# Stores of finished rows: moved from SyncE's queue to ScalarE's, with a longer pause before them

## The chip, the core and the metric

The kernel runs on one core of a Trainium2 chip. The metric is the device time of one execution in microseconds (us), the median of several runs. The engines are named as in the profile: PE is TensorE, DVE is VectorE, ACT is ScalarE, POOL is GpSimd, and SP is SyncE, which computes nothing and here only issues DMAs.

## What is computed

The input `x` holds 4 sequences of 3584 rows with 192 channels. Three layers follow each other:

```python
out = einsum('hk,bskhg->bshg', softmax(weight), x_windows)   # causal filter, 7 taps, 8 heads of 24 channels
skip = x @ w_skip > 0                                        # only these rows pass the first expert layer
e = argmax(x @ w_gate); y = gate * (relu(x @ w1[e]) @ w2[e]) # 8 experts, 192 -> 1024 -> 192
x[skip] = x[skip] + y[skip]
e2 = argmax(x @ w_gate2 + modality_bias[modality_id])        # second expert layer, every row
out = gate2 * (relu(x @ w1b[e2]) @ w2b[e2])
```

## The kernel before

The 14336 rows are cut into 128 tiles of 112 rows, and 16 tiles make a group, so there are eight groups (`NG`). **Phase 1** works on the groups one after the other. For each group and each of the 8 heads TensorE multiplies the input with a band matrix (`filt`); ScalarE scales the result into the tile `hl` as f16 (`conv`, line 711), and VectorE adds the low part that the f16 lost (`lows`, line 724). TensorE transposes pairs of tiles (`tr`), ScalarE copies them to SBUF as `xtb`, and a second matmul (`gm`) gives the gate logits. When all logits of a group are there, `fin` (line 767) computes the expert codes and the gate factors on GpSimd and VectorE, with one exponential on ScalarE, and writes factors and row numbers into spare columns of `hl`. Then `store` (line 794) sends `hl` to the DRAM tensor `rows`, 112 partitions with 16 rows of 792 bytes each, 1386 KB a group.

`hl` is allocated in `conv` with `bufs=4`: the first conv of group g+4 writes into the buffer of group g and must wait until that group's store has read it.

**After and beside phase 1**, `route_a` turns the codes into lists of rows per expert, on VectorE, GpSimd and TensorE. `prep` splits the expert weights into f16 high and low parts on ScalarE and VectorE and writes them to DRAM; its lane 1 takes its SBUF from the memory that phase 1 gave back. `Ffn.run` then works through blocks of 128 rows of one expert: an indirect gather from `rows` (GpSimd), a DMA transpose (`xpose`, SP), two matmul stages, with `hh` (ScalarE) and `hlo` (VectorE) between them. Blocks of the first layer that need only groups 0 to 3 start while groups 5 to 7 still pass `fin` and `route_a`.

**The order of the work** is written out by hand. Every side job is a Python generator; `Tasks.tick` (line 98) advances each of them by one schedule step, and `yield n` means that the generator goes on n steps later. Phase 1 counts v from 0 to 75; in each v it makes a transpose, a `lows`, one step of all side jobs, a conv and a `gm`, and then a second step of the side jobs. `fin(g)` is added at v = 8g+19. During the blocks, `bg` (line 1292) gives the steps, two per call and four calls per block at first. For ScalarE, VectorE, TensorE and GpSimd the wrapper `InOrder` fixes the instructions in the order in which the program issues them. SP has no such wrapper: the scheduler may place its DMAs in another order.

```python
class Core:
    def __init__(self, tc):
        self.raw = tc.nc
        self.vector, self.scalar = InOrder(tc, tc.nc.vector), InOrder(tc, tc.nc.scalar)
        self.tensor, self.gpsimd = InOrder(tc, tc.nc.tensor), InOrder(tc, tc.nc.gpsimd)
```

Line 70 of the profile is the call inside `InOrder`, so nearly all instructions of the four engines carry it. Numbers such as conv(g,h) mean group and head.

Of the kernel before, what the change touches and what calls it, by code (L numbers as in the profile page):

```python
# [10 lines left out]
I32 = mybir.dt.int32  # L11
# [12 lines left out]
TP = 112  # L24
# [3 lines left out]
GT = 16  # L28
# [29 lines left out]
def f32v(t):  # L58
    return t.rearrange("p t c -> p (t c)").bitcast(F32).rearrange("p (t c) -> p t c", c=RW // 2)
# [600 lines left out]
class Phase1:  # L660
# [106 lines left out]
    def fin(self, g):  # L767
        nc, m, p = self.nc, self.m, self.p2
        t0 = g * GT
        L, hl, (s, inv) = self.L.pop(g), self.hl.pop(g), self.sc.pop(g)  # L770
        meta = f32v(hl)
        nc.gpsimd.tensor_copy(meta[:, :, MB + 2], inv[:TP, 0:1].to_broadcast([TP, GT]))
        nc.gpsimd.tensor_copy(meta[:, :, MB + 3], m.modf[:, t0:t0 + GT])
        nc.gpsimd.tensor_copy(meta[:, :, MB + 4], m.ids[:, t0:t0 + GT])
        nc.gpsimd.memset(meta[:, :, MB + 5], 0.0)
        sc17 = p.tile([TP, 17], F32, name="sc17")
        nc.gpsimd.tensor_tensor(sc17, m.gsi[:TP], inv[:TP, 0:1].to_broadcast([TP, 17]), ALU.mult)
        nc.gpsimd.tensor_tensor(L, L, sc17.unsqueeze(1).to_broadcast([TP, GT, 17]), ALU.mult)
        nc.gpsimd.tensor_tensor(L[:, :, 9:17], L[:, :, 9:17], m.bias[:, t0:t0 + GT, :], ALU.add)
        yield 4  # L780
        cd = p.tile([TP, GT, 2], F32, name="cd")
        gt = p.tile([TP, GT, 2], F32, name="gt")
        for w in m.gate(nc.gpsimd, L[:, :, 1:17].rearrange("p t (m e) -> p t m e", m=2), GT, 2, p, cd, gt, 2, 3, 1):
            yield w
        yield 1
        nc.vector.scalar_tensor_tensor(m.code[:TP, 0, t0:t0 + GT], L[:, :, 0], 0.0, cd[:, :, 0], ALU.is_gt, ALU.mult)
        nc.vector.scalar_tensor_tensor(m.code[:TP, 1, t0:t0 + GT], L[:, :, 0], 0.0, cd[:, :, 1], ALU.is_le, ALU.mult)
        nc.gpsimd.tensor_copy(meta[:, :, MB], gt[:, :, 0])
        nc.gpsimd.tensor_tensor(meta[:, :, MB + 1], gt[:, :, 1], inv[:TP, 0:1].to_broadcast([TP, GT]), ALU.mult)
        self.codes = g + 1  # L790
        yield 2
        self.store(g, meta)

    def store(self, g, meta):
        t0 = g * GT
        self.nc.sync.dma_start(self.rows[t0 * 128 + 128:(t0 + GT) * 128 + 128, :].rearrange("(p t) c -> p t c", p=128)[:TP], meta.bitcast(I32))

    def run(self, tk, tkw, tables):
        for g in range(2):
# [601 lines left out]
```

## Time and profile before

| what | value |
|---|---|
| median of 3 runs | 1024.06 us (1023.78 to 1024.61) |
| the profiled execution | 1022.52 us |
| its span in the trace | 1020.7 us |
| PE busy | 947.0 us (93%) |
| DVE busy | 640.6 us (63%) |
| ACT busy | 455.4 us (45%) |
| POOL busy | 523.9 us (51%) |
| mean granted TensorE clock | 0.969 |

The span runs from the first to the last recorded instruction; the execution's own time has 1.8 us more around it. Shares over the whole span mix phase 1 with the long stretch of blocks behind it, so stretches are read one by one. A granted clock of 1.00 is 2.4 GHz, 0.50 is 1.2 GHz.

### The profile page before, as it was taken

What the parts mean: (1) busy time and instruction counts of PE and PEld (TensorE: products, weight loads), DVE (VectorE), ACT (ScalarE), POOL (GpSimd) and SP (SyncE); (2) the same over time, 40 slices, a digit from 0 to 9 for tenths busy, and PEclk for the clock granted to TensorE, in tenths of its full rate; (3) what the DMA queues carried; (4) which work ended last, traced back from release to release, by engine and by line L of the source; (5) the groups of instructions that cost most, each with busy time, mean ns of one, the idle gap of its engine ahead of it and who ended that gap; (6) DMA issues with size and microseconds to landing.
All of it is one profiled execution on the core that took longest, in us unless ns stands there. A gap on an engine that the chain in (4) does not pass through costs nothing. (4 is left out here: it accounts for less than half of the span.)

```text
span 1020.7 us, 30001 instructions
## 1 busy us (share of the span) xinstructions
PE 947.0 (93%) x11512; PEld 881.3 (86%) x11512; DVE 640.6 (63%) x1742; ACT 455.4 (45%) x833; POOL 523.9 (51%) x1027
## 2 busy tenths in 40 slices
PE   5998968999999799998999999999999999999994
PEld 3666757989999789998889999998898999999994
DVE  6699975989989998875445555558633333333331
ACT  2786641525555334433355555543233333333331
POOL 4055788444443233344277877854354555555532
PEclk9999869999999999999899999999999999999997
DMA  8394768667888596669933434342276322223231
GB/s 290 146 336 184 236 218 229 194 199 206 238 253 231 154 316 192 187 187 283 304 77 105 107 88 120 97 112 68 55 245 174 72 71 75 73 76 75 75 96 45
DMA packets 109145, 165.53 MB, mean 162 GB/s; under 512 B 80975, under 2 KB 86073, under 8 KB 103232
## 3 DMA queue, kind: packets, MB, share of 16 engines
q1 hardware_dynamic: 94368, 134.02, 42.6%
q0 software_dynamic: 13920, 28.87, 11.7%
q8 instruction: 92, 1.51, 0.6%
q10 hardware_dynamic: 704, 0.63, 0.2%
q14 instruction: 61, 0.50, 0.2%
HBM read 181.56 MB, written 58.42 MB: 235 GB/s over the span
## 5 line engine op out<-in xcount | busy, mean ns | idle before, releaser
L70 PEld LDWEIGHTS <-w1b 128*128 128x128 f16 x4840 | 370.7, 99 | 35.4 <-issue 9.0
L70 DVE SCALAR_TENSOR_TENSOR ws<-bank,ws 128x512 f16<-128x512 f32 x220 | 151.9, 691 | 252.7 <-ACT ws L70 250.0
L70 PE MATMUL bank<-xp,w1b 128*128 128x256 f16 x2200 | 262.5, 273 | 3.1 <-DMA xp<-gt 2.0
L70 PEld LDWEIGHTS <-ws 128*128 128x128 f16 (+2 forms) x3088 | 248.1, 98 | 8.7 <-issue 2.2
L70 PE MATMUL bank<-w2b,ws 128*128 128x192 f16 x2640 | 239.2, 246 | 0.0
L70 POOL DMA_INDIRECT out_dram<-u,si x114 | 115.2, 1010 | 168.9 <-ACT u L70 109.2
L70 ACT ACTIVATE ws<-bank 128x512 f16<-128x512 f32 x220 | 130.6, 597 | 118.7 <-PE bank L70 117.9
L70 PE MATMUL bank<-xt,w1b 128*128 128x128 f16 x2640 | 167.7, 224 | 7.6 <-DVE hlo L70 4.4
L70 ACT ACTIVATE hh<-bank 128x512 f16<-128x512 f32 x132 | 78.2, 593 | 154.8 <-PE bank L70 148.3
L70 PE MATMUL bank<-w2b,hh 128*128 128x192 f16 x1056 | 140.7, 249 | 3.4 <-DMA w2b<-s2a 3.4
L70 PE MATMUL bank<-w2b,hlo 128*128 128x192 f16 x528 | 131.4, 249 | 0.0
L70 DVE SCALAR_TENSOR_TENSOR hlo<-bank,hh 128x512 f16<-128x512 f32 x132 | 90.0, 685 | 49.0 <-ACT hh L70 48.6
L70 POOL DMA_INDIRECT gt<-rows,idxs x44 | 48.2, 1096 | 137.0 <-issue 116.0
L70 ACT ACTIVATE u<-bank,c 128x192 f32<-128x192 f32 x114 | 47.9, 420 | 145.9 <-PE bank L70 121.3
L70 PEld LDWEIGHTS <-hh 128*128 128x128 f16 x1056 | 96.0, 101 | 4.1 <-issue 3.7
L70 POOL DMA_INDIRECT gt<-rows,idx x64 | 63.8, 997 | 28.2 <-issue 15.5
L70 POOL DMA_INDIRECT gt<-rows,idxB x56 | 55.9, 998 | 26.9 <-issue 12.5
L70 PE MATMUL bank<-xg,band 128*112 128x384 f32 x128 | 60.0, 559 | 4.2 <-DVE hl L70 4.2
L70 POOL TENSOR_TENSOR xs<-gt 128x128 f32<-128x128 f16 x124 | 53.6, 457 | 6.7 <-DVE x2s L70 4.8
L70 PE MATMUL bank<-ob,oa 128*128 128x56 f16 (+2 forms) x446 | 49.8, 263 | 5.1 <-DVE ob L70 3.9
L70 ACT COPY xtb<-bank 128x672 f16<-128x672 f16 x64 | 45.9, 720 | 16.7 <-PE bank L70 16.4
L70 PEld LDWEIGHTS <-hlo 128*128 128x128 f16 x528 | 52.2, 99 | 0.1
(242 smaller groups left out, 1182.7 us busy)
## 6 DMA issues: line engine op xcount, KB each, us to landing
w1b<-s1b SPq DMA_DIRECT2D x59, 1024.0 KB
w2b<-s2b SPq DMA_DIRECT2D x59, 768.5 KB
ws<-in_moe_w_dram SPq DMA_DIRECT2D x16, 768.0 KB
rows<-hl SPq DMA_DIRECT2D x8, 1386.0 KB
xg<-in_x_dram SPq DMA_DIRECT2D x7, 1536.0 KB
ws<-in_moe_w_dram SPq DMA_DIRECT2D x16, 512.0 KB
ws<-in_moe_w_dram SPq DMA_DIRECT2D x32, 256.0 KB
s1a<-w1b SPq DMA_DIRECT2D x8, 1024.0 KB
```

The source lines that it names most:

```text
L70: r = f(*args, **kw)
```

## The change

The store of a group's finished rows is issued on ScalarE's DMA queue instead of SP's, and `fin` pauses six schedule steps before it instead of two.

```diff
@@ -788,12 +788,12 @@
         nc.gpsimd.tensor_copy(meta[:, :, MB], gt[:, :, 0])
         nc.gpsimd.tensor_tensor(meta[:, :, MB + 1], gt[:, :, 1], inv[:TP, 0:1].to_broadcast([TP, GT]), ALU.mult)
         self.codes = g + 1
-        yield 2
+        yield 6
         self.store(g, meta)
 
     def store(self, g, meta):
         t0 = g * GT
-        self.nc.sync.dma_start(self.rows[t0 * 128 + 128:(t0 + GT) * 128 + 128, :].rearrange("(p t) c -> p t c", p=128)[:TP], meta.bitcast(I32))
+        self.nc.scalar.dma_start(self.rows[t0 * 128 + 128:(t0 + GT) * 128 + 128, :].rearrange("(p t) c -> p t c", p=128)[:TP], meta.bitcast(I32))
```

## Rows read from the trace of the kernel before

**Rows 1.** Stretches: from:to, length, busy us (count) of five engines, clock, DMA share, GB/s.

```profile
95.00:111.00 16.00, 13.98 (x165) 10.72 (x163) 15.37 (x45) 11.90 (x22) 10.51 (x33) 1.00 0.48 150
142.00:165.00 23.00, 17.61 (x202) 16.84 (x202) 16.15 (x47) 4.27 (x9) 20.28 (x64) 0.79 0.86 249
180.00:1020.00 840.00, 799.66 (x9860) 766.40 (x9857) 503.96 (x1338) 357.01 (x665) 415.99 (x714) 0.99 0.52 147
```

**Rows 2.** The source view of line 796: issue in ns min/median/max, first and last start.

```profile
L796 SPq DMA_DIRECT2D rows<-hl x8: 319/327/346, 57.8 to 164.4; - x8
```

**Rows 3.** Waits of SP's queue up to 200 us: total us, times, longest us.

```profile
SPq L796 <- POOL hl L70: 47.8, 7, 16.2
...
SPq L302 <- DVE w1b L70: 14.5, 3, 9.7
...
SPq L296 <- DMA rows<-hl: 3.4, 1, 3.4
```

**Rows 4.** Waits of TensorE's matmuls from 140 to 182 us, same columns.

```profile
PE bank L70 <- DVE cuma L70: 4.6, 2, 3.5
...
PE bank L70 <- DMA xt<-gt: 1.2, 1, 1.2
```

**Rows 5.** The tile view of `hl`: all convs, durations in ns, first and last start.

```profile
L70 ACT ACTIVATE hl<-bank,s x64: 571/580/632, 12.6 to 123.0; 112x384 f16<-112x384 f32 x64
```

**Rows 6.** Timeline of ScalarE, convs (3,5), (4,0), (4,5), (5,0), (5,5), (6,0): start, duration.

```profile
60.37 0.58 ACT L70 ACTIVATE hl<-bank,s 112x384 f16<-112x384 f32 x1
...
65.02 0.62 ACT L70 ACTIVATE hl<-bank,s 112x384 f16<-112x384 f32 x1
...
72.59 0.58 ACT L70 ACTIVATE hl<-bank,s 112x384 f16<-112x384 f32 x1
...
80.19 0.58 ACT L70 ACTIVATE hl<-bank,s 112x384 f16<-112x384 f32 x1 [1.17 <-DMA rows<-hl]
...
90.50 0.58 ACT L70 ACTIVATE hl<-bank,s 112x384 f16<-112x384 f32 x1
...
94.93 0.63 ACT L70 ACTIVATE hl<-bank,s 112x384 f16<-112x384 f32 x1
```

**Rows 7.** Timeline of SP's queue: stores 1, 2, and 4 with 5.

```profile
71.94 0.33 SPq L796 DMA_DIRECT2D rows<-hl  x1
...
85.52 0.33 SPq L796 DMA_DIRECT2D rows<-hl  x1
...
118.42 16.92 SPq L796 DMA_DIRECT2D rows<-hl  x2
```

**Rows 8.** Stretches of half a microsecond, columns as in rows 1.

```profile
91.00:91.50 0.50, 0.50 (x9) 0.26 (x8) 0.50 (x3) 0.50 (x2) 0.00 (x0) 1.00 0.06 25
91.50:92.00 0.50, 0.50 (x14) 0.50 (x10) 0.50 (x2) 0.50 (x2) 0.40 (x1) 1.00 0.00 0
```

**Rows 9.** Timeline at the start: a DMA issue on ScalarE's queue.

```profile
2.15 0.45 ACTq L70 DMA_DIRECT2D rA<-in_moe_modality_id_dram  x1
```

**Rows 10.** Timeline of VectorE: `lows` after convs (4,0), (5,0) and (6,0).

```profile
66.85 0.60 DVE L70 SCALAR_TENSOR_TENSOR hl<-bank,s,hl 112x384 f16<-112x384 f32 x1
...
80.80 0.62 DVE L70 SCALAR_TENSOR_TENSOR hl<-bank,s,hl 112x384 f16<-112x384 f32 x1 [0.54 <-ACT hl L70]
...
96.70 0.60 DVE L70 SCALAR_TENSOR_TENSOR hl<-bank,s,hl 112x384 f16<-112x384 f32 x1
```

**Rows 11.** Timeline of ScalarE: the routing copies behind the places of stores 6 and 7.

```profile
151.38 0.17 ACT L70 COPY offa<-bank 128x16 f32<-128x16 f32 x1 [4.99 <-PE bank L70]
...
164.90 0.17 ACT L70 COPY offa<-bank 128x16 f32<-128x16 f32 x1 [1.17 <-PE bank L70]
```

**Rows 12.** Timeline of GpSimd: its last write into `hl` for groups 6 and 7.

```profile
149.74 0.22 POOL L70 TENSOR_TENSOR hl<-gt,s 112x16 f32<-112x16 f32 x1
...
164.11 0.21 POOL L70 TENSOR_TENSOR hl<-gt,s 112x16 f32<-112x16 f32 x1
```

**Rows 13.** Timeline of TensorE: the first weight matmuls of lane 1.

```profile
174.50 0.62 PE L70 MATMUL bank<-ws 128*128 128x128 bf16 x8 [1.71 <-POOL qa L70]
```

## The prediction

> **What bounds the kernel now.** I read the stretches first [rows 1]. From 180 us to the end TensorE is busy for 799.66 of 840 us at a granted clock of 0.99, so whatever moves the start of that stretch moves the end one for one. No store of the change lies there: SP issues the eight stores between 57.8 and 164.4 us [rows 2]. Before it, from 95 to 111 us, VectorE is busy for 15.37 of 16 us and ScalarE for only 11.90; from 142 to 165 us GpSimd is the fullest engine, 20.28 of 23 us. So the front is paced by VectorE and then by chains between GpSimd and VectorE, and a store matters only where one of these, or what feeds them, waits for it.
>
> Second, the waits of SP's queue [rows 3]. SP stands 47.8 us before stores, seven times, waiting for GpSimd's last write into `hl`. That is the price that the change takes away. But SP computes nothing, so I asked what stands behind a store. In the conv stage it is loads that wait for their own buffers anyway, at line 302 for up to 9.7 us. Behind store 5 it is the first transpose of a gathered block: TensorE later waits 1.2 us for it, but in the same stretch it waits 3.5 us for VectorE's `cuma`, which comes from the GpSimd chain [rows 4]. The 1.2 us would only lengthen that wait.
>
> **Where the stores go.** `fin(g)` gets its first tick as the second tick of v = 8g+19. Its pauses up to the store add to 4+2+3+3+1+1+2 = 16 ticks, two per v: the store falls after conv(g+3,3). With 6 in place of 2 it falls two v later, after conv(g+3,5). SP is free to take its issues in another order; on ScalarE the wrapper fixes this place. Ring and place work together: `hl` has four buffers, so conv(g+4,0), three convs later, needs store g landed. I name convs by counting the 64 of the tile view, eight per group, back from the last at 123.0 us [rows 5]. The trace shows this wait: conv(5,0) at 80.19 us ended 1.17 us of idleness with the landing of store 1 [rows 6].
>
> **Prices.** *Landing.* Two bounds. Store 2 was issued at 85.52 us [rows 7]; its last bytes moved in the slice up to 91.5 us, none after [rows 8]: 6.0 us with little beside it. Store 1, issued at 71.94 us [rows 7] behind other transfers, landed when conv(5,0) began, at 80.19 us: 8.25 us. *Issue.* A DMA issue on ScalarE's queue took 0.45 us [rows 9], a store on SP 0.33 [rows 2]. ScalarE pays at the stores; SP's saving is worth nothing, since SP waits.
>
> **Group 4.** conv(3,5) starts at 60.37 us and takes 0.58 [rows 6], so store 0 is issued at 60.95 us and lands at 66.95 to 69.2. conv(4,0) began at 65.02 [rows 6]; now it can't begin before the landing. VectorE took up its result at 66.85 [rows 10], 1.2 us after the conv's end (65.02 + 0.62): this is the cover. The new start on VectorE is landing + 0.62 = 67.6 to 69.8, a delay of 0.7 to 3.0 us. Neither store is the nearer one, so I take the middle, a landing of 7.1 us: +1.8. The issue's 0.45 us lies inside this wait.
>
> **Group 5.** conv(4,5) at 72.59 + 0.58 + 1.8 of shift puts store 1 at 74.97 us. With 7.1 us again it lands at 82.1; conv(5,0) started at 80.19, so the total shift is +1.9. There is no cover here: VectorE was idle 0.54 us for this conv [rows 10].
>
> **Group 6.** conv(5,5) at 90.50 + 0.58 + 1.9 puts store 2 at 92.98 us. The DMA engines are as free there as in rows 8, so 6.0 us: 98.98. conv(6,0) would start at 94.93 + 1.9 = 96.83, so ScalarE is held 2.15 us. VectorE's start at 96.70 leaves 1.2 us of cover [rows 6, 10]; +1.0 comes through. Total +2.9.
>
> **Group 7 and the rest.** The same order holds for group 7, and the cover of 1.2 us, as in groups 4 and 6, should take what is left once the convs run late: 0; without it some 1 us. Store 4 has no conv behind it in the ring: 0. Store 5 falls between weight scalings of `prep`, at about the time at which SP's issue of it ended, 118.42 + 16.92 = 135.34 us [rows 7]; only the 0.45 us issue is new, with the GpSimd chain as cover, and 0.45 without it. Store 6 falls behind the second `hh` of block 0, where ScalarE then idles 4.99 us up to 151.38 [rows 11]; GpSimd's write is done at 149.74 + 0.22 [rows 12], so wait and issue are over by 150.4. Store 7 falls behind the second `hh` of block 2; its GpSimd write ends at 164.32 [rows 12], the issue at 164.77, and the next ScalarE instruction ran at 164.90 after an idle wait for TensorE [rows 11]: 0. If GpSimd came later by 1 us, that copy, and the routing matmuls behind it, would wait for the store by as much.
>
> **Sum.** +1.8 +0.1 +1.0 = +2.9 us at the end of the conv stage, carried to the end. The profiled execution took 1022.52 us (span 1020.7 and 1.8 around it); the sum gives 1025.4. The median of the runs is 1024.06, 1.5 above that execution, so I forecast 1026.9 us. With 6.0 us throughout the steps give +0.7, -0.3 and +0.7 in total after groups 4, 5 and 6; with 8.25 us in groups 4 and 5 +3.0, +4.2 and +5.2: 1024.8 to 1029.3. A measurement here can tell about 0.2%, 2.05 us, from no change: slower begins at 1026.1, faster ends at 1022.0.
>
> **The rivals.** *Faster: the stores land early.* On a queue of its own a store need not stand behind SP's backlog, nor SP's transfers behind a store. The point that decides is a landing in 5.0 us: then group 4's conv result is there at 60.95 + 5.0 + 0.62 = 66.6, before VectorE's 66.85, group 6's at 96.7, just in time, and no ring wait costs anything. Group 5's 0.54 us of VectorE idleness goes. At the other end an SP weight load waited 3.4 us for a store's landing [rows 3], and TensorE then sat idle 1.71 us before the weight matmuls at 174.50 us [rows 13]; an earlier landing of store 7 gives that back. Together -2.2: 1021.8 us. For it: store 1's 8.25 us contain a queue. Against it: store 2 took 6.0 us with little beside it. Chance 0.20.
>
> The Trainium skill, "DMA: Bandwidth & Descriptors", section "Queues, rings and completion order", says that each DMA engine takes packets in turn from all queues that have work. By that rule this rival would hold in group 5, where store 1 would share with the backlog rather than follow it. No row here shows two such queues at work on large transfers, so by the trace its chance stays as above.
>
> *No change.* The shift is real but GpSimd takes it up: if its own backlog sets the pace later, a late conv costs nothing. For it: 20.28 of 23 us busy [rows 1]. Against it: from 95 to 111 us GpSimd is busy only 10.51 of 16 us, so it waits for others where the delay arises. Here belongs too that the landings are near the lower end: +0.7 is inside the limit. 1024.1 to 1026.1 us, chance 0.33.
>
> *Slower by more.* The stalls thin out TensorE's work and its clock falls once more. From 142 to 165 us it is granted 0.79 [rows 1], which between 2.4 and 1.2 GHz means 42% of 23 us, 9.7 us, at the lower level. One more such spell delays matmul work by up to half of it, 4.8 us, on top of the forecast: 1031.7 us, chance 0.07.
>
> *The change does less than it says.* If the store waited for GpSimd anyway, the pause would be empty. For stores 6 and 7 it is; stores 1 and 2 left SP at 71.94 and 85.52 us, when GpSimd was done, 1.2 and 5.6 us ahead of the new places, so there it is not.
>
> **How the numbers follow.** The forecast has 0.40, slower by more 0.07, no change 0.33, faster 0.20; so slower 0.47, same 0.33, faster 0.20. The range leaves out half of the faster case, below 1021.8, and the clock case, above 1030.0.
>
> **What would show it.** Right: ScalarE waits for `rows<-hl` before conv(4,0), conv(5,0) and conv(6,0), 1 to 4 us each; the last conv ends 2 to 4 us after 123; stores on ScalarE's queue at about 61, 75 and 93 us; the dense stretch starts later by as much. Wrong: no such waits, or landings under 5 us; or the waits are there and the dense stretch starts where it did, which would make GpSimd the pace; or the time moves within the dense stretch, which no step here explains.

## The result, and the profile after

The changed kernel takes 1031.68 us (median of 20 runs, 1027.0 to 1037.8), the kernel before, on the same chip, 1025.46 us (20 runs, 1022.26 to 1029.65). The ratio is 1.0053, with a 95% interval of 1.0038 to 1.0068: on 1024.06 us that is 5.4 us slower, 3.9 to 7.0. (The two medians themselves are 6.2 us apart; the ratio is what the text uses.) Forecast were 2.9 us, and a range up to 1030.0 us, which the median exceeds. The direction was right and the size too small. The profiled execution took 1030.55 us (span 1028.7).

The same three stretches as in [rows 1], same columns:

```profile
95.00:111.00 16.00, 14.39 (x177) 11.22 (x176) 15.12 (x48) 13.08 (x24) 10.26 (x32) 1.00 0.39 124
142.00:165.00 23.00, 15.95 (x159) 15.24 (x159) 14.46 (x36) 4.35 (x9) 19.97 (x50) 0.57 0.87 261
180.00:1020.00 840.00, 804.70 (x9910) 770.67 (x9910) 503.86 (x1339) 358.17 (x666) 421.79 (x728) 0.99 0.54 149
```

The dense stretch is as dense as before, at the same clock of 0.99. So the time is lost ahead of it, as a later start. (The lower clock from 142 to 165 us, 0.57 against 0.79, is taken up at the end of the experiments.) The first gather of the second row list shows it, in the tile view of `rows` (count, durations in ns, first and last start), before:

```profile
L70 POOL DMA_INDIRECT gt<-rows,idxs x44: 979/982/2247, 196.7 to 429.5; - x44
```

and after, 7.4 us later, 8 with the span's end:

```profile
L70 POOL DMA_INDIRECT gt<-rows,idxs x44: 980/985/2245, 204.1 to 436.9; - x44
...
L70 ACTq DMA_DIRECT2D rows<-hl x8: 310/311/337, 60.1 to 171.3; - x8
```

(Two single executions differ by 8.0 us here; the runs' ratio says 5.4.) Where the delay arises is read from ScalarE's timeline after. The lines are conv(3,5), store 0, conv(4,0), conv(4,5), store 1, conv(5,0), store 2, conv(5,5) and conv(6,0), against [rows 6]:

```profile
60.00 0.58 ACT L70 ACTIVATE hl<-bank,s 112x384 f16<-112x384 f32 x1
60.06 0.34 ACTq L70 DMA_DIRECT2D rows<-hl  x1
...
66.87 0.58 ACT L70 ACTIVATE hl<-bank,s 112x384 f16<-112x384 f32 x1 [2.07 <-DMA rows<-hl]
...
72.25 0.67 ACT L70 ACTIVATE hl<-bank,s 112x384 f16<-112x384 f32 x1
72.60 0.33 ACTq L70 DMA_DIRECT2D rows<-hl  x1
...
83.83 0.58 ACT L70 ACTIVATE hl<-bank,s 112x384 f16<-112x384 f32 x1 [4.22 <-DMA rows<-hl]
...
95.28 0.31 ACTq L70 DMA_DIRECT2D rows<-hl  x1
...
96.05 0.58 ACT L70 ACTIVATE hl<-bank,s 112x384 f16<-112x384 f32 x1
...
101.68 0.58 ACT L70 ACTIVATE hl<-bank,s 112x384 f16<-112x384 f32 x1 [1.04 <-PE bank L70]
```

Read the distances, not the clock times, since two executions are shifted against each other. From conv(3,5) to conv(4,5) it is 12.25 us; in [rows 6] 12.22. The 2.07 us wait for store 0 is made up within five convs. From conv(4,5) to conv(5,0) it is 11.58 us against 7.60: here 4.0 us are lost, to store 1, which took 11.2 us to land. From conv(5,0) to conv(5,5) it is 12.22 us against 10.31: another 1.9.

Those 1.9 us are TensorE's. VectorE takes up the late conv at 84.44 us:

```profile
84.44 0.62 DVE L70 SCALAR_TENSOR_TENSOR hl<-bank,s,hl 112x384 f16<-112x384 f32 x1 [3.59 <-ACT hl L70]
...
85.49 0.21 DVE L70 TENSOR_TENSOR eia<-t1a,bank 128x56 f32<-128x56 f32 x1
```

`eia` of `route_a` is queued behind it on VectorE, and `eia` is what TensorE's wait before the 24 matmuls of the next input scaling ended with:

```profile
85.76 2.72 PE L70 MATMUL bank<-xg 128*128 128x128 bf16 x24 [3.87 <-DVE eia L70]
```

They took 2.72 us; in the trace before the same group ran like this:

```profile
82.11 1.53 PE L70 MATMUL bank<-xg 128*128 128x128 bf16 x24 [0.61 <-DVE eia L70]
```

The stretches give the reason. Columns as in rows 1; first before:

```profile
58.00:60.00 2.00, 2.00 (x29) 1.44 (x27) 1.97 (x6) 2.00 (x5) 1.68 (x8) 1.00 0.82 253
60.00:66.00 6.00, 5.13 (x63) 3.67 (x61) 5.93 (x19) 5.64 (x11) 3.23 (x10) 1.00 0.88 291
66.00:72.00 6.00, 6.00 (x81) 4.45 (x80) 5.75 (x19) 4.69 (x9) 4.58 (x17) 1.00 0.99 387
...
85.00:92.00 7.00, 5.75 (x67) 4.11 (x66) 6.69 (x21) 5.77 (x10) 3.51 (x15) 1.00 0.59 203
110.00:118.00 8.00, 7.91 (x59) 5.28 (x58) 7.72 (x25) 4.56 (x9) 6.33 (x18) 0.57 0.97 329
```

then after:

```profile
58.00:60.00 2.00, 2.00 (x26) 1.26 (x23) 1.97 (x6) 2.00 (x5) 1.37 (x6) 1.00 0.00 0
60.00:66.00 6.00, 5.13 (x60) 3.56 (x57) 5.93 (x18) 4.80 (x10) 3.54 (x10) 1.00 0.86 276
66.00:72.00 6.00, 6.00 (x81) 4.46 (x80) 4.71 (x15) 5.13 (x10) 3.56 (x13) 1.00 1.02 331
...
85.00:92.00 7.00, 6.24 (x48) 5.12 (x48) 4.39 (x17) 2.52 (x5) 4.57 (x21) 0.54 0.11 44
110.00:118.00 8.00, 7.03 (x78) 5.53 (x77) 7.86 (x23) 5.66 (x12) 4.38 (x13) 1.00 0.84 282
```

After TensorE's 3.87 us of idleness the granted clock is 0.54 from 85 to 92 us, close to the 1.2 GHz level; before it was 1.00. A dip that the kernel before has at 110 to 118 us (0.57) is missing after, so part of this may be given back; that is argued, not tested. Measured from conv(3,5), conv(6,0) is 7.1 us late, and the last conv (126.98 us against 122.96) 4.4.

The last two columns, DMA share and GB/s, hold the start of the story. From 58 to 60 us the DMA engines move nothing, because store 0 has not left. By 72 us they have moved 3.64 MB since 58 us (0 + 6 x 0.276 + 6 x 0.331), against 4.57 MB before. Store 1 meets 0.93 MB more backlog, 2.3 us at 0.40 MB per us. And SP no longer stands in front of a store until GpSimd is done, so it issues the weight load of line 296 at 66.97 us, ahead of store 1, where before it came 4.0 us behind it, at 75.93 us. The load is 512 KB, 0.52 MB, by the same estimate another 1.3 us. SP's timeline before, with the load of the next input (`xg`) ahead of the weight load:

```profile
75.53 0.34 SPq L678 DMA_DIRECT2D xg<-in_x_dram  x1
75.93 1.42 SPq L296 DMA_DIRECT2D ws<-in_moe_w_dram  x1
```

and after:

```profile
66.97 0.61 SPq L296 DMA_DIRECT2D ws<-in_moe_w_dram  x1
75.92 0.34 SPq L678 DMA_DIRECT2D xg<-in_x_dram  x1
```

### The profile page after: what moved, and what is told of

The parts are those of the page before. It is cut to its first block, busy times and chain, and to the rows that moved or that the text cites. A ratio compares the mean times of both kernels' runs of the same rounds, so it can differ in the third digit from the quotient of the medians.

```text
span 1028.7 us, 29992 instructions
## 1 busy us (share of the span) xinstructions
PE 950.3 (92%) x11512; PEld 884.5 (86%) x11512; DVE 638.8 (62%) x1742; ACT 455.3 (44%) x833; POOL 523.2 (51%) x1027
```

## Experiments

The measure of lateness is the distance from conv(3,5) to conv(5,0) on ScalarE, 19.82 us in [rows 6]; the columns "late", "store 1" (issue to conv(5,0)) and "weight load" (issue of line 296's load, counted from store 1's issue; 4.0 us in the kernel before) come from one profiled execution each. That of e9 was the slowest of its twelve runs, those of e4 and e6 the fastest. Each ratio is to the kernel before on the same chip. Where conv(5,0) waited for something else, store 1's landing was no later than the column says; e17's lateness is that of the last repeat.

| kernel | store 1, us | weight load, us | conv(5,0) late, us | ratio to before [95%] |
|---|---|---|---|---|
| changed kernel | 11.2 | -5.6 | 4.0 | 1.0053 [1.0038, 1.0068] |
| e1 queue only | 9.8 | -4.2 | 1.6 | 1.0052 [1.0028, 1.0077] |
| e2 pause only | 8.4 | 4.0 | 0.1 | 1.0012 [0.9988, 1.0035] |
| e3 changed, five buffers | no wait | -5.4 | -1.1 | 1.0005 [0.9990, 1.0021] |
| e4 before, five buffers | no wait | 13.3 | -1.2 | 1.0002 [0.9978, 1.0025] |
| e5 all but store 1 | 9.7 | 0.4 | 2.9 | 1.0054 [1.0029, 1.0079] |
| e6 store 1 alone | 7.3 | 3.3 | -0.2 | 1.0006 [0.9983, 1.0030] |
| e7 changed, SP held | 11.2 | 0.3 | 4.5 | 1.0048 [1.0023, 1.0073] |
| e8 stores 4 to 7 | 8.4 | 4.0 | 0.2 | 1.0000 [0.9974, 1.0025] |
| e9 store 0 alone | 11.1 | 0.4 | 3.7 | 1.0028 [1.0005, 1.0050] |
| e10 all but store 0 | 8.5 | 3.3 | 0.9 | 1.0036 [1.0008, 1.0064] |
| e11 stores 2 and 3 | 8.5 | 4.0 | 0.3 | 1.0002 [0.9978, 1.0026] |
| e12 short pause for store 0 | 10.7 | -4.9 | 3.1 | 1.0048 [1.0024, 1.0072] |
| e13 stores 0 and 1 | 10.0 | -6.0 | 3.0 | 1.0066 [1.0045, 1.0087] |
| e14 stores 2 to 7 | 8.0 | 4.0 | -0.3 | 1.0028 [1.0006, 1.0051] |
| e15 short pause, SP held | 10.0 | -0.4 | 2.5 | 1.0051 [1.0026, 1.0076] |
| e16 store 0, queue only | 9.2 | 4.0 | 1.0 | 1.0039 [1.0017, 1.0060] |
| e17 conv(5,0) made late | untouched | 4.0 | 4.5 | 1.0065 [1.0039, 1.0091] |
| e18 conv(4,0) made late | untouched | 3.7 | 0.4 | 1.0003 [0.9979, 1.0026] |

**Queue or pause, and the ring (e1 to e4).** e1 undoes the pause, e2 makes the pause alone, e3 gives the changed kernel a fifth `hl` buffer, e4 the kernel before. In e3 and e4 the first part of a later tile is halved for room.

```diff
-        yield 6
+        yield 2
```

> The stores go to ScalarE's queue, the pause stays at 2 steps. Ring theory (a conv that reuses a buffer of hl waits for the store's landing, and store 1 lands late because its queue no longer stands in front of SP's other transfers): store 1 can leave only when GpSimd is done, about 72 us, as in the changed kernel (72.6), so it lands at 82 to 84 us again, conv(5,0) starts 2 to 4 us late, and group 4 and 6 have no wait. On top, ScalarE is held before GpSimd's last writes of groups 1, 5, 6 and 7, up to 4 us each: in all 3 to 10 us slower than before. Theory that ScalarE's issue slots and the late chain of stores 5 to 7 cost the time, not the ring: 5 us or more slower, with conv(5,0) no later than 81 us.

```diff
-        yield 2
+        yield 6
```

> The pause is 6 steps, the stores stay on SP. Ring theory with both parts at work: stores 0 and 2 leave 3 to 5 us later than before and land after conv(4,0) and conv(6,0) want the buffer, store 1 leaves at 72 to 73 us and lands in 8 to 9 us in SP's order: 1 to 3 us slower than before. If the queue alone is the cause: no change, within 1 us.

```diff
-XA = 16
+XA = 8
-            self.hl[g] = self.p3.tile([TP, GT, RW], F16, name="hl", bufs=4)
+            self.hl[g] = self.p3.tile([TP, GT, RW], F16, name="hl", bufs=5)
```

> The changed kernel with five buffers for hl in place of four (room is made by a smaller x2a, 8 columns in place of 16, as in e4). Ring theory: no conv waits for a store, TensorE does not go idle at 82 to 85 us, and the time equals that of e4 within 1.5 us. Theory that ScalarE's issue slots or the late chain cost the time: still 4 to 6 us above e4.

> The kernel before with five buffers for hl and the smaller x2a: the base for e3. Ring theory: the wait of 1.2 us before conv(5,0) goes, half a microsecond of it was VectorE's; the smaller x2a may cost or give a little at its own place. Within 2 us of the kernel before.

The ring is the way in which the change costs time: with five buffers ScalarE never waits for `rows<-hl`, TensorE doesn't stop, and the change costs nothing that can be measured. The stretch of e3 that answers to TensorE's gap (1.89 us busy in the changed kernel):

```profile
80.00:85.00 5.00, 5.00 (x64) 4.26 (x63) 4.90 (x18) 2.41 (x5) 2.98 (x12) 1.00 1.02 396
```

The pause alone shows nothing in the time (1.0012): in e2 SP's stores stay in the same order, and leave when GpSimd is done, not 3 to 5 us later as expected. The queue without the pause costs as much as the change, but in another way too. ScalarE then stands in front of its next work until GpSimd has written `hl`. e1's waits of ScalarE (total us, times, longest):

```profile
ACT xtb L70 <- POOL hl L70: 8.5, 3, 4.9
ACT hh L70 <- POOL offa L70: 6.3, 1, 6.3
ACT hh L70 <- POOL hl L70: 4.4, 1, 4.4
```

The changed kernel has none of these three waits. So the pause keeps ScalarE from standing, but in the time nothing of it is seen: 1.0053 with it, 1.0052 without.

**Which store (e5 to e8).** My first theory was that store 1, the longest wait, is itself the cause. e5, e6 and e8 choose by group which stores are changed, the queue together with its pause; in e7 SP issues, at the store's old place, a 792-byte copy out of `hl`, so that it waits for GpSimd as before.

This is e5 against the changed kernel; in e6 the condition for SP is `g != 1`, in e8 `g < 4`:

```diff
-        yield 6
+        yield 2 if g == 1 else 6
...
-        self.nc.scalar.dma_start(self.rows[t0 * 128 + 128:(t0 + GT) * 128 + 128, :]
+        eng = self.nc.sync if g == 1 else self.nc.scalar
+        eng.dma_start(self.rows[t0 * 128 + 128:(t0 + GT) * 128 + 128, :]
```

> Store 1 as in the kernel before (SP, 2 steps), the other seven as in the changed kernel. Ring theory with store 1 as the main loss: conv(5,0) begins near 81 us, TensorE has no idle stretch near 82 to 85 us, and what is left are the short waits of groups 4, 6 and 7: 0 to 2.5 us slower than before. If the loss is spread over all stores or sits in ScalarE's issues: 4 us or more slower.

> Store 1 alone as in the changed kernel (ScalarE, 6 steps), the others as before. Ring theory with store 1 as the main loss: issued at 72 to 73 us, landing 10 to 11 us later, conv(5,0) begins near 83 us after a wait of 3 to 4 us, and the time is 3 to 5 us above before. If the loss is spread: 0 to 1.5 us.

And e7 against the changed kernel:

```diff
-        yield 6
+        yield 2
+        self.nc.sync.dma_start(self.hold[g:g + 1, :], meta.bitcast(I32)[0:1, 0, :])
+        yield 4
```

> The changed kernel, and at the old place of each store SP issues a copy of one partition's first row of hl (792 bytes) into a scratch tensor, so that SP is held before GpSimd's last write as it was. If store 1 lands late because the freed SP queue puts its weight load in front (issued at 67 us in place of 76): that load goes back behind, store 1 lands some 1.3 us earlier or more, and the time falls to 2 to 4 us above before. If sharing the DMA engines with what SP has issued anyway makes it late: landing 10 us or more after the issue, 4 to 6 us above before.

> Stores 0 to 3 as before (SP, 2 steps), stores 4 to 7 as in the changed kernel. Ring theory: no conv waits for these stores, so within 1.5 us of before. Theory of the late chain: most of the 5 us stays.

The theory fell. Put back on SP, store 1 still landed late and the loss stayed (e5); changed alone, it landed sooner than before and cost nothing (e6). Store 1 suffers; it isn't the cause. Holding SP (e7) brought the weight load back to 73.29 us, 0.3 us behind store 1 and not 4.0 as before, and store 1 landed as late as ever. Stores 4 to 7 alone cost nothing that can be measured. That left stores 0, 2 and 3.

**Store 0 (e9 to e12).** The same switch; the condition for SP with the old pause is `g != 0` in e9, `g == 0` in e10 and `g not in (2, 3)` in e11. In e12 every store is on ScalarE's queue, and only the pause differs:

```diff
-        yield 6
+        yield 2 if g == 0 else 6
```

> Only store 0 changes (ScalarE's queue, six steps); all others as before. Theory (store 0 leaves about 2 us later, the DMA engines idle before it and the backlog behind it makes every later landing late): nearly the whole loss is here. Conv(4,0) starts near 67 us after a wait of 2 to 2.6 us for the landing, conv(5,0) at 82 to 83 us (80.2 in the kernel before), ratio 1.003 to 1.005, 3 to 5 us. Rival (the waits of the later groups, or the spread of ScalarE's issues, make the loss): 0 to 1.5 us, ratio up to 1.0015, though conv(4,0) waits.

> Store 0 goes as in the kernel before (SyncE, two steps), all others as in the changed kernel. Theory (store 0 is the cause): conv(4,0) without a wait near 65 us, conv(5,0) at 80 to 81 us, no clock dip between 84 and 92 us, 0 to 2 us over the kernel before, ratio 1.000 to 1.002. Rival (stores 2 and 3 or the rest make the loss): 3 to 6 us, ratio 1.003 to 1.006.

> Only stores 2 and 3 change. Theory (store 0): both land while the DMA engines are nearly free; waits before conv(6,0) and conv(7,0) of at most 1 us; 0 to 1.5 us over the kernel before, ratio up to 1.0015. Rival (the landings of stores 2 and 3, on the stretch where VectorE is the fullest engine, make the loss): 3 to 5 us, ratio 1.003 to 1.005.

> All stores on ScalarE's queue, six steps of pause, but two for store 0: it is issued near 58 us, as early as on SyncE. Theory in its first form (the later departure of store 0, that is, the pause, is the cause): conv(4,0) with a wait of at most 0.5 us, 0 to 2 us over the kernel before, ratio 1.000 to 1.002. In its second form (store 0 on ScalarE's queue lands late whenever it leaves, since it shares the DMA engines with SyncE's backlog): conv(4,0) waits 1 us or more and the loss stays at 4 to 6 us, ratio 1.004 to 1.006.

Store 0 alone makes store 1 late by the full amount, though store 1 is issued by SP as before (e9). Its ratio, 1.0028, is only about half of the change's and a little below what was expected, so the time doesn't show that store 0 makes the whole loss. And SP's order didn't stay: the weight load went ahead of the `xg` load and follows store 1 at once, as SP's timeline of e9 shows:

```profile
73.70 0.34 SPq L797 DMA_DIRECT2D rows<-hl  x1
74.14 0.78 SPq L296 DMA_DIRECT2D ws<-in_moe_w_dram  x1
77.03 0.33 SPq L678 DMA_DIRECT2D xg<-in_x_dram  x1
```

With store 0 untouched, conv(5,0) comes only 0.9 us late (e10), as the theory has it, but e10's ratio lies above what it allowed: not settled. Stores 2 and 3 alone cost nothing that can be measured. e12 fell between its two forms: store 0 left on time, at 58.17 us, and conv(4,0) had no wait, as in the first; but store 1 took 10.7 us and the ratio is 1.0048, as in the second. So store 0's longer pause isn't needed for the loss.

**Settling it (e13 to e18).** e13 and e14 split the stores, with SP for `g >= 2` and for `g < 2`. e15 is e7 with e12's short pause, e16 puts store 0 alone on ScalarE's queue with the old pause:

```diff
-        yield 4
+        if g:
+            yield 4
```

```diff
-        self.nc.sync.dma_start(self.rows[t0 * 128 + 128:(t0 + GT) * 128 + 128, :]
+        eng = self.nc.scalar if g == 0 else self.nc.sync
+        eng.dma_start(self.rows[t0 * 128 + 128:(t0 + GT) * 128 + 128, :]
```

> Stores 0 and 1 on ScalarE's queue after six steps, stores 2 to 7 as in the kernel before. Theory (the whole loss arises where stores 0 and 1 pass the backlog): conv(4,0) waits 2 to 2.6 us, conv(5,0) starts at 82.5 to 84.5 us, ratio 1.004 to 1.006, 4 to 6 us. Rival (part of the loss comes from the later stores): the same waits, but ratio 1.001 to 1.003.

> The complement: stores 0 and 1 as in the kernel before, 2 to 7 on ScalarE's queue after six steps. Theory: conv(4,0) and conv(5,0) as in the kernel before (5,0 near 80 to 81 us), waits of at most 1 us before conv(6,0) and conv(7,0), ratio 0.999 to 1.0015. Rival (the later stores make part of the loss): ratio 1.002 to 1.004.

> All stores on ScalarE's queue, store 0 after two steps, the others after six, and SyncE held at the old places by a 792-byte copy out of hl. Store 0 then leaves on time and the weight load of line 296 stays behind store 1, so both suspected causes are gone while the queue remains changed. Theory (each of the two alone makes store 1 late): conv(4,0) without a wait, store 1 lands within 7 to 8.5 us of its issue, conv(5,0) at 80 to 81 us, ratio 1.000 to 1.002. Rival (ScalarE's queue itself, with store 0 on it, is what delays store 1): store 1 takes 10 us or more, conv(5,0) at 82.5 us or later, ratio 1.004 to 1.006.

> Store 0 alone on ScalarE's queue, with the pause of the kernel before (two steps); all else as before. Theory A (backlog: store 0 leaving late, or the weight load of line 296 going ahead of store 1): store 0 leaves on time and SyncE still issues store 1 itself, ahead of the weight load, so store 1 lands within 8.5 us, conv(5,0) at 80 to 81 us, ratio 1.000 to 1.0015. Theory B (the switch of store 0's queue is enough): store 1 takes 9.7 us or more, conv(5,0) at 82 us or later, ratio 1.003 to 1.006.

e17 and e18 repeat one conv of the kernel before and touch no store; this is e17, and e18 has `5 if (g, h) == (4, 0)`:

```diff
-        nc.scalar.activation(hl[:, :, c0:c1], pc, AF.Copy, scale=s[:TP, 0:1])
+        for _ in range(8 if (g, h) == (5, 0) else 1):
+            nc.scalar.activation(hl[:, :, c0:c1], pc, AF.Copy, scale=s[:TP, 0:1])
```

> The kernel before with conv(5,0) repeated eight times (the same result written again, 7 x 0.58 = 4.1 us more on ScalarE); no store, queue or pause is changed. Theory (a conv(5,0) ended some 4 us late is what costs the time): VectorE and TensorE idle near 81 to 85 us, the 24 matmuls of the next input scaling take about 2.7 us in place of 1.5, the granted clock drops near 85 to 92 us, ratio 1.003 to 1.006. Rival (the loss comes through the loads or the stores' own queue): ratio 1.000 to 1.002.

> The kernel before with conv(4,0) repeated five times (4 x 0.58 = 2.3 us more on ScalarE), the delay that store 0's landing causes in the changed kernel. Theory (that delay is caught up by conv(4,5), as in the changed kernel, where the distance from conv(3,5) to conv(4,5) is 12.25 us against 12.22): ratio 0.999 to 1.0015. Rival (group 4's wait carries through, as predicted with 1.8 us): ratio 1.0015 to 1.003.

e17 is the decisive one: with every store where it was, a conv(5,0) that ends 4.5 us later costs 1.0065, and its trace shows the same things in the same place. Timeline of ScalarE:

```profile
80.59 4.87 ACT L70 ACTIVATE hl<-bank,s 112x384 f16<-112x384 f32 x8 [1.38 <-PE bank L70]
```

of TensorE:

```profile
86.82 2.72 PE L70 MATMUL bank<-xg 128*128 128x128 bf16 x24 [5.09 <-DVE eia L70]
```

and the stretches:

```profile
80.00:85.00 5.00, 1.73 (x20) 1.28 (x19) 0.47 (x2) 4.18 (x8) 0.00 (x0) 0.93 0.81 305
85.00:92.00 7.00, 5.18 (x47) 4.44 (x47) 4.01 (x14) 2.89 (x6) 3.73 (x20) 0.56 0.21 71
```

The same done to conv(4,0) costs nothing (e18): five convs in a row took 3.07 us there, and conv(5,0) came 0.4 us late. So group 4 has slack and group 5 has none.

```profile
64.98 3.07 ACT L70 ACTIVATE hl<-bank,s 112x384 f16<-112x384 f32 x5
...
80.56 0.58 ACT L70 ACTIVATE hl<-bank,s 112x384 f16<-112x384 f32 x1 [0.32 <-DMA rows<-hl]
```

e13 has the whole loss with stores 0 and 1 alone (1.0066). But its complement e14 came out in the rival's range (1.0028), though conv(5,0) was not late, so the two halves add to more than the whole; that isn't explained. In e15 the rival came out: store 1 took 10.0 us with store 0 on time and SP held. But the hold didn't restore SP's order, as its timeline shows, the weight load being issued before store 1 (72.74 us) and not after the `xg` load:

```profile
72.02 0.25 SPq L792 DMA_DIRECT2D hold<-hl  x1
72.32 0.39 SPq L296 DMA_DIRECT2D ws<-in_moe_w_dram  x1
75.62 0.33 SPq L678 DMA_DIRECT2D xg<-in_x_dram  x1
```

so both forms of the theory remain for it. e16 fell between its two: 9.2 us, conv(5,0) 1.0 us late, and a ratio on theory B's side.

**What is settled, and what not.** Over the eight kernels with conv(5,0) at least 2.5 us late (the changed one, e5, e7, e9, e12, e13, e15, e17) the ratios are 1.0028 to 1.0066, 1.0052 in the mean. Over the eight with at most 0.4 us (e2, e3, e4, e6, e8, e11, e14, e18) they are 1.0000 to 1.0028, 1.0007 in the mean. The three between (e1, e10, e16; 0.9 to 1.6 us) have 1.0036 to 1.0052, more than their lateness would suggest.

The traces also show where the loss sits. From conv(3,5) to the last conv the eight late kernels take 65.0 to 68.5 us, the eight others 60.2 to 62.7. From the last conv to the first gather of the second row list the two groups are alike: 75.3 to 79.0 us and 74.6 to 78.3. There the trace before has 73.7 us, less than any other, and the one after 77.1. So the loss is complete at the end of the conv stage, and the further 3.4 us between these two traces, in which the lower clock from 142 to 165 us falls, don't go with the change.

Shown are that a late conv(5,0) by itself costs what the change costs (e17), that the ring makes it late (e3), and that moving store 0 alone makes store 1 late (e9). Open is by which way. The table has a rival to store 0's later departure that splits the kernels with four buffers without exception: where store 1 took 9.7 us or more, the weight load was issued ahead of it or at most 0.44 us behind; where it took 9.2 us or less, 3.3 to 4.0 us behind (e1's 9.8 us is only an upper bound). This covers e12 and e15, in which store 0 left on time. e12 and e16 issue store 0 alike, on ScalarE's queue 2.2 us before conv(3,5); with the load ahead of store 1 (e12) conv(5,0) is 3.1 us late, with the load in its old place (e16) 1.0. But no run moved the weight load alone, and none has store 0 late with the load in its old place, so the two aren't separated; nor did a run change the 0.93 MB of backlog alone. Open too is whether the later stores add something: stores 4 to 7, and 2 and 3, each by themselves cost nothing that can be measured (e8, e11), all six 1.0006 to 1.0051 (e14), with e10 like them.

## Why the prediction was wrong in size

- **The stage, right.** The dense stretch starts later and is otherwise as before; the loss arises in the conv stage, through the ring, in group 5 above all. The stores left at 60.06, 72.60 and 95.28 us (about 61, 75 and 93 were named), and the last conv came 4.0 us later (2 to 4 were named). "No change, GpSimd paces" fell with it.
- **The failed step: group 5's landing.** "With 7.1 us again it lands at 82.1; ... the total shift is +1.9", so +0.1 over group 4. Measured: 11.2 us to land, and conv(5,0) 4.0 us later. Both bounds, 6.0 and 8.25 us, came from stores of a trace in which store 0 left on time. I moved each store by itself and took its landing from the old surroundings. But from 60 to 84 us the DMA engines are full (shares of 0.86 to 1.02 in the stretches above), and what was queued there had changed: 0.93 MB less was moved by 72 us, and a weight load of 0.52 MB was issued 9 us earlier, by the estimates above 2.3 and 1.3 of the 4.0 us. I had priced store 0's shift at group 4 alone, and the time that SP gets back at nothing, since its loads "wait for their own buffers anyway". Which of the two makes how much isn't settled.
- **Group 4, +1.8: right wait, wrong carry.** Store 0 landed in 6.8 us (7.1 assumed), ScalarE waited 2.07 us, VectorE 0.93. But conv(4,5) was back in time, and e18 puts the price of such a delay at nothing that can be measured. I took VectorE's late start as lasting, without looking for slack in the five convs behind it.
- **Group 6, +1.0: the wait came, the loss didn't.** ScalarE idled 1.04 us before conv(6,0). The row names TensorE, but the filter matmul that feeds this conv was done at 99.33 us. All eight kernels with four buffers that move store 2 with the long pause have this wait, and their conv(6,0) starts 6.4 us after store 2's issue; no other has it, nor e3 with five buffers. So it was most likely store 2's landing (6.0 us assumed). VectorE took up the conv 6.24 us after conv(5,5), against 6.20 before: the cover of 1.2 us was enough, since store 2 left 0.8 us before conv(5,5) started and not behind its end.
- **The clock.** The dip at 85 to 92 us is the mechanism of "slower by more", and that rival's time, 1031.7 us, is near the measured one. But it priced a spell at 142 to 165 us, by half of its length. The real one sits in the conv stage, comes from the late conv(5,0), and is worth 1.9 us by conv(5,5), beside the 4.0 that caused it. So the rival's sum came out for another reason. The text's own upper sum, +5.2 us, is near the measured 5.4 by luck as well: it carried 3.0 us from group 4, which didn't last, and had store 1 land in 8.25 us.
- **Faster by early landings: fell.** The landings that a conv waited for took 6.8, 11.2 and 6.4 us in the changed kernel (store 3: 110.18 us to conv(7,0) at 116.63). On a queue of its own store 1 took 1 us less where nothing else was changed (7.3 us in e6 against 8.25), not 3, and left 0.7 us later.
- **Group 7 and stores 4 to 7 at 0.** conv(7,0) waited 0.45 us. e8 supports the zero; e14 leaves room for up to 0.5%. The issue on ScalarE took 0.31 to 0.34 us, not 0.45.

## What to carry to other kernels

Where the DMA engines are full, stores aren't priced one by one: list what is queued from the first moved transfer to the next free moment, and move the whole list. Ask too what the queue that gets free will issue sooner: here it was a weight load beside the next store. A ring's wait matters where the stage has no slack, and a late instruction deliberately put there in the old kernel (as in e17 and e18) prices that place without touching any transfer. A fifth buffer took the wait away altogether (e3) and brought the time back to that of the kernel before, not below it.

## What was not expected of the hardware

**A store on a queue of its own had half of the bytes once, and a third another time.** Stretches from the issue of store 1 to the conv behind it, e6:

```profile
72.36:79.68 7.32, 7.32 (x92) 5.99 (x91) 6.05 (x21) 4.08 (x10) 5.77 (x17) 1.00 1.01 382
```

and the changed kernel:

```profile
72.60:83.83 11.23, 8.93 (x106) 6.99 (x106) 6.98 (x22) 3.87 (x9) 6.49 (x18) 1.00 1.01 401
```

The store has 1386 KB, 1.42 MB. In e6 2.80 MB moved meanwhile (7.32 x 0.382), so it had 51%; in the changed kernel 4.50 MB, so 32%. The Trainium skill, "DMA: Bandwidth & Descriptors", section "Queues, rings and completion order", says that a DMA engine takes packets in turn from the queues with work. With packets of like size that makes an even split between two queues; e6 agrees with it, the other run doesn't, and nothing here tells why. A queue of its own isn't what tells the two apart: e9's store 1, on SP's queue, had 31% too (4.56 MB moved in 11.10 us).

**The clock did not answer alike to like pauses.** The same 24 matmuls in e10:

```profile
82.47 2.72 PE L70 MATMUL bank<-xg 128*128 128x128 bf16 x24 [1.55 <-DVE eia L70]
```

and in e16:

```profile
82.78 1.54 PE L70 MATMUL bank<-xg 128*128 128x128 bf16 x24 [1.60 <-DVE eia L70]
```

After pauses of 1.55 and 1.60 us they ran at the lower level in the one and at the full level in the other (81 to 92 us: clock 0.84 and 1.00).
